# GpSimd's sums of w_out's quarters spread over batch 1's output units, their casts some units behind, and quarter products read in front of later low parts

## The chip, the cores and the metric

One NeuronCore of a Trainium2 chip runs the whole program. The metric is the device time of one execution in microseconds. TensorE (PE in the rows) multiplies, VectorE (DVE), ScalarE (ACT) and GpSimd (POOL) do the elementwise work, and SyncE's queue (SP) issues the DMAs. Each engine works through its own queue in order; semaphores tie the queues together.

## The reference

The inputs are q, k, v of 8 batches, 8 heads, 576 tokens and 64 channels, and the weights of a gated MLP. Attention runs within chunks of 64 tokens; its output, put together to 512 channels a token, is the MLP's input x:

```python
scores = scale * q_c @ k_c^T            # chunks of 64 tokens
out    = softmax(scores) @ v_c          # -> x: (8, 576, 512)
h = gelu_tanh(x @ w_in)                 # (8, 576, 1024)
u, v = h[..., :512], h[..., 512:]
v_n = layer_norm(v) * g_ln
v_s = w_sg @ v_n + b_sg                 # over the tokens of a batch
return x + (u * v_s) @ w_out
```

## The kernel before

**Precision by pairs.** Every operand of a large product is held as a high and a low float32r part (`_h`, `_l` or hi, lo): ScalarE casts the high part, VectorE subtracts it from the source to get the low part (`split`, lines 99 to 104), and TensorE sums three products.

**Units.** A batch's MLP is cut into units of TensorE work with VectorE and ScalarE work behind each: `v_unit` (v half of x @ w_in, GELU, layer norm; 12 products of 512 columns), `u_unit` (u half, GELU into the tile u2; 24 products of 288 columns), `s_unit` (w_sg times the normed v, times u), and the output. In the name v23 the first digit is the batch and the second the number of the unit. v24 takes the first 64 tokens of batches 2 and 3 at once, from the tile xodd, and its layer norm ends in the tiles z1 and z2 (lines 548 to 550). Accumulators are the three PSUM buffers `pm`; a unit can start when one is free, that is when the GELU (or another reader) of the unit three before has run.

**Output, two ways.** Batches 0 and 1 have output units o00 to o13 (`o_unit`, lines 694 to 703), four a batch. From batch 2 on the output is formed by Strassen's scheme from seven products of quarters (`o_product`, named p1, p5, p2, p6, p3, p7, p4 in this order). Their right sides are sums of the gated activations' quarters, made in `gated_quarters`; for p6, p7 and p4 they are split into high and low parts in the tile `tv`. Their left sides ("factors") are quarters of w_out and sums of quarters. `make_factors` (the B steps) forms them once: ten additions or subtractions on GpSimd (line 254), four splits (lines 285 and 286), DMA writes to the DRAM tensor `factors` (lines 261 and 287), and four loads of the first factors into a ring of four places that takes over w_out's tiles (line 245). The sums, and the high and low parts of each split, lie in one tile `sums` that takes the place (tag "u2") that u2 has in other stages; so the first sum waits until s13 has read batch 1's u2, and the GELU of u20, which writes batch 2's u2, waits until `sums` is no longer read.

**Attention.** 36 tiles of 128 tokens: loads (A), scores (S, or P for two tiles) and softmax, transposition of the probabilities (T, on VectorE and ScalarE), output product and its eviction to xh, xl, xf (O, or Q for two; `keep`). The products of tiles 5 and up go into the fixed tile `banks` and into a `pm`. Tile 13 holds the last tokens of batch 2 and the first of batch 3.

**Order.** `START` lists the steps up to batch 2's first three units by hand; then a loop runs over the units of batches 2 to 7, and `SLOTS` says after which unit a piece of attention is traced. The framework keeps data dependences, and orders a queue by the order in which the program traces the work, save that work which it takes to be ready sooner may go ahead. `tc.keep_in_program_order` pins an instruction behind the one traced before it on its engine; all sums, their casts and the factors' writes are pinned, their low parts on VectorE are not. Small tiles share the tag "tmp" with four buffers: the GELU output hs of a v unit, the transposed blocks, the output ot of an output unit.

Of the kernel before, what the change touches and what calls it, by code (L numbers as in the profile page):

```python
# [22 lines left out]
P = 128  # L23
# [6 lines left out]
HS = S // 2  # L30
# [17 lines left out]
v13 Y2 u10 Y3 u11 Y4 u12 Y5 Y6 u13 Y7 A10 s10 A12 s11 P9 s12 s13 T9 o00 T10 P11 o01 o02 o03 Q9 A14 T11 o10 T12 o11 Q11  # L48
S13 A15 o12 T13 o13 P14 A17 B0 B1 v20 B2 v21 O13 B3 v22 B4
# [12 lines left out]
    0: "v1:O4 v3:T5 u0:T6 u1:O56 u1:S78 u3:T7 s0:T8 p7:O78 p7:S9A",  # L62
# [25 lines left out]
def block_attention_gated_mlp(ctx: ExitStack, tc: tile.TileContext, qkv, w_in, w_out, w_sg, g_ln, b_sg, out):  # L88
# [147 lines left out]
    ring, loads, carry = [], [0], []  # L236
# [4 lines left out]
    def load_factor():  # L241
        n = loads[0]
        loads[0] += 1
        if n < 7 * (B - QUARTERS_FROM):
            nc.sync.dma_start(out=factor_place(n).bitcast(F32), in_=factors[n % 7])

    def make_factors(step):

        def quarter(r, c):
            return [a[:, 2 * c : 2 * c + 2, 2 * r * P : 2 * (r + 1) * P] for a in (wout_h, wout_l)]  # L250

        def add(o, a, c, op=ALU.add):
            a, c = (x if x.dtype == F32 else x.bitcast(F32) for x in (a, c))
            tc.keep_in_program_order(nc.gpsimd.tensor_tensor(o, a, c, op=op))  # L254

        sub = lambda o, a, c: add(o, a, c, ALU.subtract)
        (h11, l11), (h12, l12), (h21, l21), (h22, l22) = (quarter(r, c) for r in range(2) for c in range(2))
        if step == 0:
            for p, parts in ((1, (h11, l11)), (2, (h12, l12)), (4, (h22, l22))):
                for a, part in enumerate(parts):  # L260
                    ins = nc.sync.dma_start(out=factors[PRODUCTS.index(p), :, a], in_=part.bitcast(F32))
                    tc.keep_in_program_order(ins)
            flat = mp.tile([P, KT, S], F32R, name="sums", tag="u2").rearrange("p a c -> p (a c)")
            carry.extend(flat[:, i * 4 * P : (i + 1) * 4 * P].rearrange("p (k e) -> p k e", k=2) for i in range(4))
            carry.append(flat[:, 8 * P : 16 * P].rearrange("p (a k e) -> p a k e", a=2, k=2))
            return
        c, d, hi, lo, both = carry
        cf, df, spare = c.bitcast(F32), d.bitcast(F32), lo.bitcast(F32)
        src = cf
        if step == 1:  # L270
            add(cf, h21, h22)
            add(spare, l21, l22)
            add(cf, cf, spare)
        elif step == 2:
            sub(cf, cf, h11)
            sub(cf, cf, l11)
        elif step == 3:
            src = df
            sub(df, h11, h21)
            sub(spare, l11, l21)  # L280
            add(df, df, spare)
        else:
            sub(cf, h12, cf)
            add(cf, cf, l12)
        tc.keep_in_program_order(nc.scalar.copy(hi, src))
        nc.vector.tensor_tensor(lo, src, hi.bitcast(F32), op=ALU.subtract)
        nc.sync.dma_start(out=factors[PRODUCTS.index((5, 6, 7, 3)[step - 1])], in_=both.bitcast(F32))
        if step == 4:
            for i in range(2):
                r = const.tile([P, KT * DM], F32R, name=f"ring_{i}", tag=f"wout_{i}")  # L290
                ring.append(r.rearrange("p (n a k e) -> p n a k e", n=2, a=2, k=2))
            for _ in range(RING):
                load_factor()

# [309 lines left out]
    def gated_quarters(b, dt):  # L604
# [16 lines left out]
        sub(eng, left, left, t1)  # L621
        if dt == 3:
            n = 2 * HS
            tv = mp.tile([P, 8, DH], F32R, name="tv", tag="v").rearrange("p a c -> p (a c)")
            places = [tv[:, i * n : (i + 1) * n].rearrange("p (k c) -> p k c", k=2) for i in range(6)]
            parts = lambda r, j: tuple(quarter_of(a, r, j) for a in (gh[b], gl[b]))
            right.update({1: parts(0, 0), 5: parts(0, 1), 2: parts(1, 0), 3: parts(1, 1)})
            right.update({p: places[2 * i : 2 * i + 2] for i, p in enumerate((6, 7, 4))})
            for p, r, j in ((6, 0, 1), (7, 0, 0), (4, 1, 0)):
                split(*right[p], quarter_of(g, r, j), nc.scalar, nc.vector)  # L630

    def o_product(b, p):
# [27 lines left out]
        if p in (1, 5):  # L660
            kept = held[p] = t("kept")
            add(kept, x(*{1: (0, 0), 5: (1, 1)}[p]))
        elif p == 2:
# [78 lines left out]
    steps["G"], steps["g"], steps["B"] = lambda k: load_w_sg(), split_w_sg, make_factors  # L742
    steps["Y"] = lambda k: o_w(k // 2, k % 2)
    for step in START.split():
        steps[step[0]](int(step[1:]))
    for b in range(2, B):
# [6 lines left out]
        for name in names:  # L753
            if name == "last":
                o_product(b - 1, 4)
                continue
            if b == 2 and name in ("v0", "v1", "v2"):
                continue
            {"v": v_unit, "u": u_unit, "s": s_unit, "p": o_product}[name[0]](b, int(name[1]))
            for f, tiles in slots.get(name, ()):  # L760
                f(*tiles)
# [44 lines left out]
```

## Time and profile before

| | |
|---|---|
| median of three runs | 526.79 us (526.65 to 527.72) |
| the profiled execution | 527.16 us, of which the span from first to last instruction is 525.2 us |
| busy in the span | TensorE 492.5 us (94%), VectorE 386.0 (73%), ScalarE 292.2 (56%), GpSimd 92.4 (18%) |
| granted clock of TensorE | 0.983 of full speed over the span |

A row of the timeline gives start, length, engine, line, operation and tiles, and in brackets how long the engine was idle before it and what ended that. A group of rows with several instructions carries "x" and their count. VectorE's and ScalarE's idle time costs nothing by itself; TensorE's does, when it is not made up.

### The profile page before, as it was taken

To read this page: it belongs to the slowest core of one execution; us is meant where nothing else is said; L and a number is where in the kernel's file an instruction comes from. 1 tells how busy PE (TensorE), PEld (TensorE's weight loads), DVE (VectorE), ACT (ScalarE), POOL (GpSimd) and SP (SyncE) were. 2 spreads that over 40 slices of the span, in tenths; PEclk is the share of its full clock that TensorE was granted. 3 is DMA by queue.
4 is the path that set the end of the run, shared out by engine and by line. 5 is a ranking of instruction groups with operands and counts; after the bars stand their busy time and mean duration, and the time that the engine had idled before them with its cause. 6 is when DMAs were issued, how large, how long until landed. Compare 5 with 4: busy or idle time off the path is not lost.

```text
span 525.2 us, 12508 instructions
## 1 busy us (share of the span) xinstructions
PE 492.5 (94%) x5172; PEld 451.8 (86%) x5172; DVE 386.0 (73%) x783; ACT 292.2 (56%) x535; POOL 92.4 (18%) x94
## 2 busy tenths in 40 slices
PE   5999999999999655999999999999999999999996
PEld 4668897999997545998999889997999889998996
DVE  7998779888767873288868886678758786667156
ACT  5897867644356565126774488328762678333220
POOL 0112000301104651102221131203111131102010
PEclk9999999999999886999999999999999999999999
DMA  8867011154376366059534824078534810082006
GB/s 336 306 176 180 1 41 54 50 137 126 113 234 180 118 213 190 1 161 273 150 95 130 279 81 124 1 235 239 140 105 129 267 54 2 1 278 94 0 2 210
DMA packets 60780, 72.28 MB, mean 138 GB/s; under 512 B 36018, under 2 KB 47794, under 8 KB 60724
## 3 DMA queue, kind: packets, MB, share of 16 engines
q1 hardware_dynamic: 60724, 71.49, 44.9%
q8 instruction: 40, 0.66, 0.5%
q14 instruction: 16, 0.13, 0.1%
HBM read 58.36 MB, written 13.11 MB: 136 GB/s over the span
## 4 chain that ended last, share of the span: by engine, by line
PE 74%; DVE 12%; ACT 6%; POOL 4%; issue 2%; DMA 1%; SPq 0%; POOLq 0%; DVEq 0%; ACTq 0%
PE pm L583 21%; PE pm L563 18%; PE pm L647 13%; PE pm L526 12%; PE pm L694 2%; POOL sums L254 2%; PE banks L396 2%; PE pm L484 2%; PE pm L185 1%; DVE sm L532 1%; DVE blocks L446 1%; ACT L529 1%; DVE xl L104 1%; ACT pt L418 1%; DVE pt L420 1%
## 5 line engine op out<-in xcount | busy, mean ns | idle before, releaser
L583 PE MATMUL pm<-wsg,v 128*128 128x288 f32 x768 | 107.5, 296 | 0.0
L583 PEld LDWEIGHTS pm<-wsg,v 128*128 128x128 f32 x768 | 103.6, 188 | 0.3
L563 PE MATMUL pm<-xh,win_l 128*128 128x288 f32 x256 | 57.4, 306 | 11.9 <-ACT xf L506 6.5
L432 POOL TENSOR_TENSOR pt<-pt,den 128x512 f32<-128x512 f32 x27 | 28.4, 1064 | 191.3 <-DVE den L431 121.1
L535 POOL TENSOR_TENSOR sm<-sm,neg_half 128x1 f32<-128x1 f32 x36 | 36.6, 1015 | 126.2 <-DVE sm L534 122.9
L563 PE MATMUL pm<-xl,win_h 128*128 128x288 f32 x256 | 56.4, 303 | 0.0
L526 PE MATMUL pm<-win_h,xl 128*128 128x512 f32 x128 | 52.4, 409 | 4.1 <-DVE xl L104 2.3
L563 PE MATMUL pm<-xh,win_h 128*128 128x288 f32 x256 | 56.2, 302 | 0.0
L563 PEld LDWEIGHTS pm<-xh,win_l 128*128 128x128 f32 x256 | 42.9, 195 | 13.4 <-ACT xf L506 6.7
L526 PE MATMUL pm<-win_h,xh 128*128 128x512 f32 x128 | 50.8, 397 | 0.0
L526 PE MATMUL pm<-win_l,xh 128*128 128x512 f32 x128 | 50.8, 397 | 0.0
L101 ACT CAST gh<-u 128x576 fp32r<-128x576 f32 x24 | 16.2, 675 | 55.3 <-DVE u L588 27.8
L563 PEld LDWEIGHTS pm<-xl,win_h 128*128 128x128 f32 x256 | 42.6, 195 | 0.0
L563 PEld LDWEIGHTS pm<-xh,win_h 128*128 128x128 f32 x256 | 42.3, 194 | 0.0
L588 DVE TENSOR_TENSOR u<-pm,u 128x576 f32<-128x576 f32 x24 | 18.1, 755 | 30.4 <-PE pm L583 19.1
L543 ACT ACTIVATE v<-hs,sm 128x512 fp32r<-128x512 f32 x32 | 23.2, 724 | 30.5 <-POOL sm L535 29.1
L647 PE MATMUL pm<-gh,ring 128*128 128x288 f32 x192 | 40.1, 294 | 0.0
L449 ACT COPY ptT<-blocks 128x512 f32<-128x512 f32 x31 | 19.0, 619 | 27.3 <-DVE blocks L446 25.7
L526 PEld LDWEIGHTS pm<-win_h,xl 128*128 128x128 f32 x128 | 24.0, 188 | 11.8 <-DVE xl L104 4.5
L647 PE MATMUL pm<-tv,ring 128*128 128x288 f32 x216 | 32.0, 297 | 1.9 <-issue 1.9
L647 PEld LDWEIGHTS pm<-tv,ring 128*128 128x128 f32 x216 | 29.7, 188 | 3.6 <-ACT tv L101 1.6
L544 DVE SCALAR_TENSOR_TENSOR v<-hs,sm,v 128x512 fp32r<-128x512 f32 x32 | 24.9, 778 | 10.0 <-ACT v L543 10.0
(145 smaller groups left out, 1047.9 us busy)
## 6 DMA issues: line engine op xcount, KB each, us to landing
ring<-factors SPq DMA_DIRECT2D x42, 512.0 KB, 4.4
qkv_t<-qkv SPq DMA_DIRECT2D x32, 512.0 KB, 4.7
qkv_t<-qkv SPq DMA_DIRECT2D x124, 64.0 KB, 3.7
out_dram<-u SPq DMA_DIRECT2D x18, 288.0 KB, 5.7
out_dram<-ot SPq DMA_DIRECT2D x14, 288.0 KB, 3.0
qkv_t<-qkv SPq DMA_DIRECT2D x3, 768.0 KB, 11.7
wsg<-w_in SPq DMA_DIRECT2D x4, 512.0 KB, 6.3
wout<-w_in SPq DMA_DIRECT2D x4, 512.0 KB, 7.7
```

The lines of the kernel that those rows point to most:

```text
L101: nc.scalar.copy(hi, src)
L254: tc.keep_in_program_order(nc.gpsimd.tensor_tensor(o, a, c, op=op))
L432: (nc.gpsimd if t > last[1] else pick(f"n{t}")).tensor_tensor(pt, pt, den.unsqueeze(2).broadcast_to([P, H, D]), op=ALU.mult)
L449: nc.scalar.copy(ptT, blocks)
L526: pin(nc.tensor.matmul(pv, a[:, kt, tok], c[:, kt, DH:], start=(i == 0), stop=(i == 11)))
L535: nc.gpsimd.tensor_tensor(rs, rs, neg_half, op=ALU.pow)
L543: nc.scalar.mul(hi, h, rs)
L544: nc.vector.scalar_tensor_tensor(lo, h, rs, hi.bitcast(F32), op0=ALU.mult, op1=ALU.subtract)
L563: pin(nc.tensor.matmul(pm[:, j, :HS], a[:, kt, dc], c[:, kt, j * HS : (j + 1) * HS], start=(i == 0), stop=(i == 11)))
L583: pin(nc.tensor.matmul(pm[:, j, :HS], a[:, dc], c[:, m, j * HS : (j + 1) * HS], start=(i == 0), stop=(i == len(ops) - 1)))
L588: nc.vector.tensor_tensor(g, pm[:, :, :HS], g, op=ALU.mult)
L647: pin(nc.tensor.matmul(pm[:, e, :HS], a[:, k, e * P : (e + 1) * P], c[:, k, :], start=starts and i == 0, stop=i == len(ops) - 1, skip_grou ...
```

## The change

START and SLOTS are reordered: `make_factors` falls into single sums (B0 to B9, one instruction each, traced from o00 to v21), the splits of the sums (C5, C6, C7, each a cast, a low part and two writes, traced after A15, A17 and O13; the fourth, of product 3, after v24), and the six writes of w_out's own quarters (K0, after v22). The high and low parts of a split are two tiles of the tag "tmp" instead of places in `sums`, and a split writes two DMAs of 256 KB where it wrote one of 512 KB. The order of the additions is the same except that the third result has a place of its own and B3 and B4 form h21+h22+l21+l22-h11-l11 in a second place.

In the loop, `split_right(7)` is traced after p1's accumulator has been read and `split_right(4)` after p5's, where all three splits were traced before p1; one subtraction moves likewise. The attention pieces behind p7 of an even batch are traced after v0 of the next batch, and tile O4 of an even batch follows v0 instead of v1.

```diff
-S13 A15 o12 T13 o13 P14 A17 B0 B1 v20 B2 v21 O13 B3 v22 B4
-v13 Y2 u10 ... s13 T9 o00 T10 P11 o01 o02 o03 Q9 A14 T11 o10 T12 o11 Q11
+... s13 T9 o00 B0 T10 P11 o01 B1 o02 B2 o03 Q9 B3 A14 T11 o10
+B4 T12 o11 Q11 S13 A15 C5 B5 o12 B6 T13 o13 P14 A17 C6 B7 v20 B8 v21 O13 C7 B9 v22 K0
...
-    0: "v1:O4 v3:T5 u0:T6 u1:O56 u1:S78 u3:T7 s0:T8 p7:O78 p7:S9A",
+    0: "v0:O4 v3:T5 u0:T6 u1:O56 u1:S78 u3:T7 s0:T8 p7:O78 p7:S9A",
...
+    def sum_step(n):
+        if n == 0:
+            flat = mp.tile([P, KT, S], F32, name="sums", tag="u2").rearrange("p a c -> p (a c)")
+            sums.extend(flat[:, i * 4 * P : (i + 1) * 4 * P].rearrange("p (k e) -> p k e", k=2) for i in range(4))
+        h11, l11, h12, l12, h21, l21, h22, l22 = (a.bitcast(F32) for a in quarters())
+        s1, s2, s3, s4 = sums
+        o, a, c, op = (
+            (s1, h21, h22, ALU.add), (s2, l21, l22, ALU.add), (s1, s1, s2, ALU.add),
+            (s2, s1, h11, ALU.subtract), (s2, s2, l11, ALU.subtract),
+            (s3, h11, h21, ALU.subtract), (s4, l11, l21, ALU.subtract), (s3, s3, s4, ALU.add),
+            (s4, h12, s2, ALU.subtract), (s4, s4, l12, ALU.add),
+        )[n]
+        tc.keep_in_program_order(nc.gpsimd.tensor_tensor(o, a, c, op=op))
+
+    def keep_factor(p, parts):
+        for a, part in enumerate(parts):
+            tc.keep_in_program_order(nc.sync.dma_start(out=factors[PRODUCTS.index(p), :, a], in_=part.bitcast(F32)))
+
+    def split_sum(p):
+        hi, lo = (
+            tmp.tile([P, S], F32R, name="fac", tag="tmp")[:, : 4 * P].rearrange("p (k e) -> p k e", k=2) for _ in range(2)
+        )
+        src = sums[(5, 6, 7, 3).index(p)]
         tc.keep_in_program_order(nc.scalar.copy(hi, src))
         nc.vector.tensor_tensor(lo, src, hi.bitcast(F32), op=ALU.subtract)
+        keep_factor(p, (hi, lo))
+        if p == 3:
...
             for _ in range(RING):
                 load_factor()
+
+    def keep_quarters(_):
+        parts = quarters()
+        for p, i in ((1, 0), (2, 2), (4, 6)):
+            keep_factor(p, parts[i : i + 2])
...
-        sub(eng, left, left, t1)
-        if dt == 3:
+        if dt == 2:
+            sub(eng, left, left, t1)
+        else:
...
-            for p, r, j in ((6, 0, 1), (7, 0, 0), (4, 1, 0)):
-                split(*right[p], quarter_of(g, r, j), nc.scalar, nc.vector)
+            split_right(6)
...
         if p in (1, 5):
             kept = held[p] = t("kept")
             add(kept, x(*{1: (0, 0), 5: (1, 1)}[p]))
+            if p == 1:
+                split_right(7)
+                left, t2 = g[:, 3, :HS], g[:, 1, HS:]
+                nc.vector.tensor_tensor(left, left, t2, op=ALU.subtract)
+            else:
+                split_right(4)
...
+            if (b, name) == (2, "v4"):
+                split_sum(3)
             for f, tiles in slots.get(name, ()):
-                f(*tiles)
+                later.append((f, tiles))
+            if name != "p7" or b % 2:
+                for f, tiles in later:
+                    f(*tiles)
+                later.clear()
```

## Rows read from the trace of the kernel before

**Rows 1.** The page of the profile, parts 1 and 2: busy time of TensorE, and the granted clock in 40 slices of 13.1 us (tenths of full speed).

```profile
PE 492.5 (94%) x5172; PEld 451.8 (86%) x5172; DVE 386.0 (73%) x783; ACT 292.2 (56%) x535; POOL 92.4 (18%) x94
...
PEclk9999999999999886999999999999999999999999
```

**Rows 2.** Whom TensorE waited for between 120 us and the end of the span; columns: us in total, times, longest.

```profile
PE pm L563 <- ACT xf L506: 6.5, 1, 6.5
PE pm L563 <- ACT u L570: 5.3, 1, 5.3
PE pm L526 <- ACT xodd L512: 4.5, 1, 4.5
...
PE pm L526 <- DVE xl L104: 1.4, 3, 1.0
PE pm L526 <- ACT pt L423: 0.7, 1, 0.7
```

**Rows 3.** Busy time of each engine in eight stretches, in this order: units v23, v24, u20, u22 and u23 of batch 2 (each from its first product to the next unit's), then the three idle times of TensorE ahead of v24, u22 and u23. Columns: length, then busy us and instructions of PE, PEld, DVE, ACT, POOL, the granted clock as a share of full speed, DMA share, GB/s.

```profile
168.66:171.57 2.91, 2.91 (x12) 2.17 (x12) 0.66 (x3) 0.00 (x0) 2.83 (x3) 1.00 1.10 327
176.17:180.62 4.45, 4.45 (x13) 3.50 (x14) 3.86 (x6) 1.17 (x2) 2.34 (x2) 0.62 0.01 2
180.62:183.81 3.19, 3.19 (x25) 3.19 (x24) 3.10 (x8) 2.96 (x6) 0.99 (x1) 1.00 0.00 0
195.74:201.01 5.27, 5.27 (x24) 5.19 (x24) 3.57 (x9) 2.92 (x4) 0.79 (x1) 0.58 0.96 315
206.51:211.54 5.03, 5.03 (x24) 5.03 (x25) 0.00 (x0) 1.84 (x4) 0.00 (x0) 0.61 0.03 6
...
171.57:176.17 4.60, 0.15 (x1) 0.00 (x0) 3.66 (x6) 2.91 (x8) 3.89 (x5) 1.00 0.73 267
189.20:195.74 6.54, 0.00 (x2) 0.00 (x1) 4.08 (x7) 2.21 (x5) 3.21 (x3) 0.82 0.77 293
201.17:206.51 5.34, 0.00 (x0) 0.00 (x0) 2.56 (x6) 4.02 (x7) 1.09 (x2) 0.73 0.73 191
```

**Rows 4.** Timeline ahead of unit v24, one engine after the other (GpSimd, ScalarE, VectorE); columns: start us, us, engine, line, operation, out<-in, idle time before it and its releaser.

```profile
167.90 2.52 POOL L254 TENSOR_TENSOR sums<-wout 128x512 f32<-128x512 f32 x2
...
171.82 0.62 ACT L285 CAST sums<-sums 128x512 fp32r<-128x512 f32 x1 [3.48 <-POOL sums L254]
...
175.72 0.41 ACT L512 CAST xodd<-xl 128x256 fp32r<-128x256 f32 x1
...
172.47 1.60 DVE L286 TENSOR_TENSOR sums<-sums 128x512 fp32r<-128x512 f32 x1 [3.15 <-ACT sums L285]
...
174.66 0.41 DVE L104 TENSOR_TENSOR xl<-pm,xh 128x256 fp32r<-128x256 f32 x1
```

**Rows 5.** Timeline ahead of units u22 and u23 (ScalarE, VectorE, SyncE's queue), columns as before.

```profile
187.26 1.26 ACT L549 CAST z<-z 64x512 fp32r<-64x512 f32 x2
...
192.53 0.62 ACT L285 CAST sums<-sums 128x512 fp32r<-128x512 f32 x1 [3.52 <-POOL sums L254]
...
205.81 1.74 ACT L570 ACTIVATE u<-pm 128x576 f32<-128x576 f32 x3
...
198.26 0.68 DVE L286 TENSOR_TENSOR sums<-sums 128x512 fp32r<-128x512 f32 x1
...
198.97 0.32 SPq L287 DMA_DIRECT2D factors<-sums  x1
```

**Rows 6.** Instructions by line: those of the tile sums (lines 254 and 286), and all of line 544; columns: count, shortest/median/longest ns, first and last start.

```profile
L254 POOL TENSOR_TENSOR sums<-sums,wout x3: 1607/1608/1712, 174.2 to 187.9; 128x512 f32<-128x512 f32 x3
...
L286 DVE TENSOR_TENSOR sums<-sums x4: 680/692/1602, 172.5 to 198.3; 128x512 fp32r<-128x512 f32 x4
...
L544 DVE SCALAR_TENSOR_TENSOR v<-hs,sm,v x32: 711/752/1761, 35.7 to 487.1; 128x512 fp32r<-128x512 f32 x32
```

**Rows 7.** Timeline of the places that the moved work comes to (GpSimd, VectorE, TensorE, ScalarE), columns as in rows 4.

```profile
125.21 2.56 POOL L432 TENSOR_TENSOR pt<-pt,den 128x512 f32<-128x512 f32 x2 [20.90 <-DVE den L430]
...
166.89 1.04 POOL L432 TENSOR_TENSOR pt<-pt,den 128x512 f32<-128x512 f32 x1 [2.01 <-DVE den L431]
...
126.79 0.75 DVE L592 TENSOR_TENSOR gt<-pm,u 128x576 f32<-128x576 f32 x1
...
128.28 0.76 DVE L104 TENSOR_TENSOR gl<-gt,gh 128x576 fp32r<-128x576 f32 x1
...
129.14 0.43 PE L694 MATMUL pm<-gl,wout 128*128 128x288 f32 x2
...
164.00 0.63 ACT L423 ACTIVATE pt<-pt 128x512 f32<-128x512 f32 x1
164.92 0.72 ACT L543 ACTIVATE v<-hs,sm 128x512 fp32r<-128x512 f32 x1 [0.29 <-POOL sm L535]
```

**Rows 8.** DMAs of the tensor factors, from issue to landing.

```profile
DMA to landing us min/median/max: 2.6/4.2/8.8
```

**Rows 9.** Timeline of batch 3's quarter products (VectorE, TensorE), and TensorE's wait ahead of v51.

```profile
286.76 0.75 DVE L104 TENSOR_TENSOR tv<-u,tv 128x576 fp32r<-128x576 f32 x1
287.43 0.75 DVE L653 TENSOR_TENSOR kept<-pm,xf 128x576 f32<-128x576 f32 x1
...
288.28 1.83 PE L647 MATMUL pm<-tv,ring 128*128 128x288 f32 x12 [0.61 <-issue]
...
358.87 0.39 PE L526 MATMUL pm<-win_h,xl 128*128 128x512 f32 x1 [0.67 <-ACT pt L423]
```

More of the change, by code (lines that the diff above doesn't have):

```diff
@@ L47 @@
 v02 x1 X2 v03 X3 v04 u00 x2 g0 g1 u01 x3 g2 P5 g3 u02 g4 T5 u03 T6 s00 P7 Q5 s01 s02 T7 T8 s03 v10 Q7 v11 Y0 v12 Y1
-v13 Y2 u10 Y3 u11 Y4 u12 Y5 Y6 u13 Y7 A10 s10 A12 s11 P9 s12 s13 T9 o00 T10 P11 o01 o02 o03 Q9 A14 T11 o10 T12 o11 Q11
-S13 A15 o12 T13 o13 P14 A17 B0 B1 v20 B2 v21 O13 B3 v22 B4
+v13 Y2 u10 Y3 u11 Y4 u12 Y5 Y6 u13 Y7 A10 s10 A12 s11 P9 s12 s13 T9 o00 B0 T10 P11 o01 B1 o02 B2 o03 Q9 B3 A14 T11 o10
+B4 T12 o11 Q11 S13 A15 C5 B5 o12 B6 T13 o13 P14 A17 C6 B7 v20 B8 v21 O13 C7 B9 v22 K0
 """
@@ L235, in block_attention_gated_mlp @@
     factors = nc.dram_tensor("factors", (7, P, 2, 2, 2 * P), F32).ap()
-    ring, loads, carry = [], [0], []
+    ring, loads, sums = [], [0], []
     def factor_place(n):
@@ L245, in load_factor @@
             nc.sync.dma_start(out=factor_place(n).bitcast(F32), in_=factors[n % 7])
[L247 to L284, printed above, removed]
@@ new lines, in quarters @@
+    def quarters():
+        return [
+            a[:, 2 * c : 2 * c + 2, 2 * r * P : 2 * (r + 1) * P] for r in range(2) for c in range(2) for a in (wout_h, wout_l)
+        ]
+    def sum_step(n):
[11 more added lines that the diff above has]
+        tc.keep_in_program_order(nc.gpsimd.tensor_tensor(o, a, c, op=op))
@@ L285, in make_factors @@
+    def keep_factor(p, parts):
[6 more added lines that the diff above has]
+        src = sums[(5, 6, 7, 3).index(p)]
         tc.keep_in_program_order(nc.scalar.copy(hi, src))
         nc.vector.tensor_tensor(lo, src, hi.bitcast(F32), op=ALU.subtract)
-        nc.sync.dma_start(out=factors[PRODUCTS.index((5, 6, 7, 3)[step - 1])], in_=both.bitcast(F32))
@@ L288, in make_factors @@
-        if step == 4:
+        keep_factor(p, (hi, lo))
+        if p == 3:
             for i in range(2):
@@ L628, in gated_quarters, with split_right @@
             right.update({p: places[2 * i : 2 * i + 2] for i, p in enumerate((6, 7, 4))})
-            for p, r, j in ((6, 0, 1), (7, 0, 0), (4, 1, 0)):
-                split(*right[p], quarter_of(g, r, j), nc.scalar, nc.vector)
+            split_right(6)
+    def split_right(p):
+        split(*right[p], quarter_of(u2[0], *{6: (0, 1), 7: (0, 0), 4: (1, 0)}[p]), nc.scalar, nc.vector)
     def o_product(b, p):
@@ L741, in block_attention_gated_mlp @@
     steps["D"] = keep_clock
-    steps["G"], steps["g"], steps["B"] = lambda k: load_w_sg(), split_w_sg, make_factors
+    steps["G"], steps["g"], steps["B"] = lambda k: load_w_sg(), split_w_sg, sum_step
+    steps["C"], steps["K"] = split_sum, keep_quarters
     steps["Y"] = lambda k: o_w(k // 2, k % 2)
@@ L745, in block_attention_gated_mlp @@
         steps[step[0]](int(step[1:]))
+    later = []
     for b in range(2, B):
```

## The prediction

> **What bounds the kernel now.** I read the page first, then TensorE's waits, then the stretches around them. TensorE is busy in 94% of the span and the granted clock is full except in three slices between 170 and 210 us [rows 1]. From 120 us on TensorE has only three long waits, one each of 4.5, 6.5 and 5.3 us; the rest are below 1 us [rows 2]. All three lie in batch 2's first units. So the bound is TensorE's work everywhere but there, and there it is a chain through the sums.
>
> Ahead of v24: GpSimd starts its first sums at 167.90; ScalarE has idled 3.48 us when it can cast the first at 171.82; VectorE has idled 3.15 us when it can form the low part at 172.47, and that takes 1.60 us [rows 4]. Queued behind these two are tile 13's second low part (174.66) and the cast into xodd (175.72), for which v24 waits [rows 2, 4]. Ahead of u22 ScalarE again stands 3.52 us before a cast of a sum (192.53), and behind it are the copies to xf that free the accumulator [rows 2, 5]. Ahead of u23 the wait is for the GELU of u20, 205.81: it writes u2, which has the place of `sums`, and the last read and write out of `sums` start at 198.26 and 198.97 [rows 2, 5].
>
> The idle times are 4.45, 6.54 and 5.34 us, together 16.33 (the first stretch of 4.60 us holds 0.15 of TensorE work) [rows 3]. Each is followed by a unit at a granted clock of 0.58 to 0.62 of the full 2.4 GHz, that is partly at 1.2 GHz: v24 takes 4.45 us where v23 took 2.91, u22 5.27 and u23 5.03 where u20 took 3.19 [rows 3]. That costs 1.54 + 2.08 + 1.84 = 5.46 us more. **What can be won here is 16.33 + 5.46 = 21.8 us**, out of 527.16 us of the profiled execution. That execution is 0.37 us above the median of 526.79; I take differences and set them against the median.
>
> **Part 1: sums and casts moved.** Five of ten sums now stand before the softmax of tile 13, two behind it, and B7, B8 and B9 behind that of tiles 14 and 15, whose last multiplication starts at 166.89 on GpSimd [rows 7]. A sum takes 1.26 us (two in 2.52) to 1.7 [rows 4, 6]. So the first two results are there well ahead of their casts C5 and C6. The third is ready about 167.9 + 1.6 = 169.5, and C7's cast is pinned behind the xodd casts and no longer in front of them. With nothing to wait for, tile 13's second high part, low part and xodd casts follow v22's GELU at about 168.4 and end near 170.5; v23 ends at 171.57 [rows 3]. So v24's wait goes, and with it its slow clock. The small wait ahead of v23 (the largest of the three in the row for xl, 1.0 us) has another cause, casts and table loads of softmax and GELU on ScalarE, and stays.
>
> What is late next is u22, because u20's GELU still waits for `sums`. Times from v24's start T: v24 2.91, u20 and u21 3.19 each, two pieces of attention about 2.2 (from 187.0 to 189.20), so TensorE reaches u22 at T + 11.5 [rows 3]. The last split is pinned behind v24's z casts. These ended at 188.52, 7.90 us after v24's last product at 180.62 [rows 3, 5]. If that lag stays, the split's cast (0.62), low part (0.69) and the GELU (0.65) end at T + 2.91 + 7.90 + 1.96 = T + 12.8, a wait of 1.3 us. Bounds: the lag held 1.0 us of a slow instruction of line 544 (1761 ns against a median of 752) beside sums on GpSimd, and further such ones; without them the wait is 0 [rows 6]. But VectorE was busy without a pause from the end of that first low part, 174.07, and in the new order starts this backlog at 172.47 - 3.15 = 169.32, 4.75 us earlier, while v24 moves by 4.6 and is over 1.54 sooner; C7's low part, as slow as the one it replaces (1.60), comes into the run, and with one low part of 0.69 fewer the z casts end at 184.7, the GELU at 186.6: a wait of 3.5 [rows 4 to 6]. I take the middle, **1.8 us**. The clock after it: full after a wait of 1.0 us (v23: 1.00), 0.62 after 4.45 [rows 2, 3]. 1.8 is nearer the first: 0, at most 2.1. u23 then needs u21's accumulator, whose GELU follows at once: 0.
>
> **Part 2: what the moved work meets.** (a) B0 is pinned behind a multiplication that ends at 127.77 and, after s13's read of u2 (126.79 to 127.54), runs to 129.05. Beside it stands the low part of s13's result, 128.28, which o00 reads at 129.14 [rows 7]. VectorE's low part of a sum beside a sum on GpSimd took 1602 ns against 680 [rows 6]. If it starts only when B0 ends it is done at 129.8: **0.7 us** of TensorE wait; bounds 0 and 0.9. The Trainium skill ("SBUF — State Buffer", section "Who interferes with whom") says that a VectorE instruction with two SBUF inputs and a GpSimd instruction that reads SBUF exclude one another for the whole instruction, whichever starts first. By that rule these 0.7 us are due; without it the sum would be 0.7 us lower. The other sums among the output units lie beside instructions of VectorE that read an accumulator; I cost them at nothing. (b) C6's cast, 0.62 us, comes into ScalarE's row between the exponential at 164.00 and v20's scaling at 164.92, with 0.29 us of slack, ahead of v21's GELU and the cast for v23: **0.4 us**; bounds 0 and 0.62 [rows 5, 7]. (c) Eight tiles more in the four tmp buffers, each held until its write has landed (2.6 to 8.8 us, median 4.2) [rows 8]. C7's pair can hold back the transposed blocks of tiles 14 and 15, which TensorE reads between u21 and u22. Bounds 0 and 4.2; its writes should land near 178, and TensorE needs the blocks near 181, so I take **0.7 us**. (d) SyncE's queue: 14 writes instead of 10, and C5's pair waits there for its low part with the loads for tiles 16 and 17 behind. These are needed only at S78, behind u21: nothing. The reads of the ring start some 15 us before p1 in the new order: nothing.
>
> **Part 3: the loop.** In an odd batch p6 waits 0.61 us instead of 0.16 because VectorE reads p1's accumulator, which p6 goes on with, at 287.43, behind a low part (286.76) that the change traces later [rows 9]. Putting the read in front gives 0.45 us in each of batches 3 and 5: 0.9. The low parts moved behind have p5, p2 and more in front of p7: nothing. The waits ahead of v51 (0.67) and for tile 22's and 31's low parts (1.4 in all less v23's 0.95) lie where O and S pieces move [rows 2, 9]. They may go or return elsewhere: 0.3 of 1.1. Gain **1.2**, bounds 0 and 2.0.
>
> **The sum.** 21.8 - 1.8 - 0.7 - 0.4 - 0.7 + 1.2 = 19.4 us: 526.8 - 19.4 = **507.4 us**. All costs at nothing and all gains: 21.8 + 2.0, or 503.0.
>
> **Rivals.** (1) *The wait moves to u22 in full.* v24's layer norm and the last split queue behind tmp buffers or behind B8 and B9 on GpSimd, and u20's GELU comes as late after TensorE's arrival as a wait of before: 6.54 us and 2.08 of slow clock instead of 1.8 [rows 3]. Then 507.4 + 6.8 = 514.2. For it: VectorE has no pause in that stretch, and the last sums can't start before 167.9 [rows 4, 7]. Against: the cast no longer waits behind the sums one after another.
>
> (2) *The spreading doesn't reach v24.* C7's cast or low part is queued ahead of the xodd chain all the same, since low parts aren't pinned, and the sums that it needs end no earlier than before's first. v24's wait and slow clock come back, 6.0 us: 513.4. Against: the pin on ScalarE.
>
> (3) *Slower: the four tmp buffers fill.* Each v unit's GELU would wait for a split's write to land, with its write held on SyncE's queue behind another split's low part, and TensorE would stop at each of v20 to v24 for 4.2 us and then run at the low clock for 1.5 more [rows 3, 8]: 28 us lost against 21.8 won, 533 us. It decides from the fourth such stop on. Against: in the rows a v unit holds its buffer a few microseconds only, and three units' accumulators cover a late GELU.
>
> (4) *No change:* the waits go but all of it is given back before the end. In batches 3 to 7 TensorE has nothing but waits below 1 us [rows 2], so nothing there can take it back.
>
> **How the numbers follow.** My forecast, 503 to 511 us, has 0.64; rival 1 0.18; rival 2 0.10; slower 0.04; no change 0.02; still faster than 503 0.02. The range of 503.0 to 515.0 takes in the forecast with its bounds and rivals 1 and 2. Within 0.2% is about what a measurement of this kernel can't tell from no change. Faster 0.94, within 0.2% 0.02, slower 0.04.
>
> **What would show it.** Right: no wait of TensorE for xodd ahead of v24; a single wait of 0 to 3.5 us between u21 and u23, ended by u20's GELU; the granted clock full from 160 to 210 us; a wait below 1 us in o00; p6 of batches 3 and 5 waiting 0.2 us. Wrong: a wait for xodd or a GELU of over 4 us, clock shares near 0.6 after it, new waits among o00 to v23 of over 2 us together, or a wait of v20 to v24 for a tmp buffer.

## The result, and the profile after

The changed kernel takes **519.27 us** (median of 4 runs, 519.05 to 519.73), the kernel before in the same session 527.25: a ratio of 0.9849, 95% interval 0.9832 to 0.9866. The change is faster by 1.5%. The forecast was 507.4 us with a range of 503.0 to 515.0: the sign was right, the size was not. About 8 us were gained where 19.4 were forecast. Line numbers shift between the two kernels: in after the attention product (484 before) is L481, units v, u and s are L523, L560 and L580, the GELU of v (529) is L526, the scores (396) L393, the sums L265, the casts and low parts of sums L277 and L278.

Parts 1 and 2 of the page, as in [rows 1]: TensorE is a little busier in its share, and the granted clock still falls in three slices.

```profile
PE 491.1 (95%) x5172; PEld 451.6 (87%) x5172; DVE 385.6 (75%) x783; ACT 288.9 (56%) x533; POOL 90.8 (18%) x94
PEclk9999999999999888999999999999999999999999
```

TensorE's waits between 120 us and the end, as in [rows 2]: us in total, times, longest.

```profile
PE pm L481 <- ACT ptT L451: 5.9, 2, 4.9
PE pm L481 <- ACT hs L526: 2.9, 2, 1.5
PE pm L523 <- ACT hs L526: 2.5, 1, 2.5
PE pm L647 <- ACT ptT L446: 1.2, 2, 0.6
PE pm L580 <- ACT u L567: 0.5, 2, 0.3
```

All three waits of [rows 2] above 4 us are gone, as forecast: nothing waits for xodd or a GELU of u20 any more, and for xf only one product of attention, 0.45 us. In their place stand two that the sum did not have: 4.9 us inside a piece of attention (for the transposed blocks of tile 15) and 2.5 us ahead of v22. Next, the stretches, with the columns of [rows 3]: the wait ahead of v22, then v22, v23, v24 and u20, the wait for tile 15's blocks, the pieces of attention behind it, u22, and u23.

```profile
166.59:169.06 2.47, 0.00 (x0) 0.00 (x0) 1.66 (x5) 2.44 (x5) 1.46 (x2) 1.00 0.92 191
169.06:173.53 4.47, 4.47 (x13) 3.52 (x14) 4.47 (x10) 3.04 (x8) 4.34 (x5) 0.62 0.96 280
173.53:176.30 2.77, 2.77 (x13) 2.23 (x12) 2.12 (x4) 1.73 (x3) 1.93 (x2) 1.00 0.05 20
176.30:179.10 2.80, 2.80 (x13) 2.26 (x12) 2.77 (x8) 0.60 (x1) 0.76 (x1) 1.00 0.73 258
179.10:182.30 3.20, 3.20 (x25) 3.19 (x24) 2.86 (x7) 2.95 (x6) 1.15 (x2) 1.00 1.02 339
186.29:191.19 4.90, 0.00 (x0) 0.00 (x0) 2.52 (x6) 3.98 (x9) 0.00 (x0) 0.92 0.77 278
191.19:194.38 3.19, 3.19 (x97) 2.93 (x97) 0.84 (x2) 1.20 (x3) 0.00 (x0) 0.50 0.96 316
194.38:198.94 4.56, 4.56 (x27) 4.56 (x25) 3.63 (x6) 3.66 (x6) 0.00 (x0) 0.69 1.07 216
198.94:202.14 3.20, 3.20 (x26) 3.20 (x25) 2.05 (x7) 2.24 (x3) 1.71 (x2) 1.00 0.04 8
```

v24 follows v23 without a gap and takes 2.80 us at the full clock. But v22 takes 4.47 us, 1.67 more than v24, and from 191.19 to 198.94 the clock costs some 1.5 (3.19 us for 96 products, of which 94 take 1.62 at the full clock in the run "split behind tile 15" below) and 1.36 (u22's 4.56 against u23's 3.20) more: 2.9. So up to batch 2's first s unit the change puts in 2.48 + 1.67 + 4.90 + 2.9, and 1.41 of two small waits at the product of tiles 11 and 12 (149.16 and 150.91): 13.4 us. It takes out the 21.8 of the forecast and the 0.95 ahead of v23: 9.4 net. By the traces this unit starts at 202.14, before at 211.54, with 0.32 between the two at the start of the multiplications of tiles 9 and 10 on GpSimd (125.53 and 125.21): 9.72. From there to the end after takes 315.4 us, before 313.7: the loop loses 1.7.

**Ahead of v22.** ScalarE and VectorE, columns as in [rows 4].

```profile
163.98 0.63 ACT L420 ACTIVATE pt<-pt 128x512 f32<-128x512 f32 x1 [2.93 <-DVE pt L417]
165.96 0.63 ACT L420 ACTIVATE pt<-pt 128x512 f32<-128x512 f32 x1 [1.35 <-DVE pt L417]
166.50 0.60 ACT L277 CAST fac<-sums 128x512 fp32r<-128x512 f32 x1
...
168.41 1.09 ACT L526 ACTIVATE hs<-pm 128x512 f32<-128x512 f32 x2
...
143.19 2.44 DVE L453 COPY ptT<-blocks 32x256 f32<-32x256 f32 x2 [0.74 <-ACT ptT L446]
...
156.08 0.68 DVE L278 TENSOR_TENSOR fac<-sums,fac 128x512 fp32r<-128x512 f32 x1
...
160.23 1.50 DVE L453 COPY ptT<-blocks 32x256 f32<-32x256 f32 x2 [0.69 <-ACT ptT L446]
...
162.54 0.68 DVE L404 TENSOR_REDUCE nmax<-banks 128x8 f32<-128x512 f32 x1
```

The same of the kernel before, v20's GELU and the maximum of tile 14's scores:

```profile
162.09 0.60 ACT L529 ACTIVATE hs<-pm 128x512 f32<-128x512 f32 x1
...
158.65 0.68 DVE L407 TENSOR_REDUCE nmax<-banks 128x8 f32<-128x512 f32 x1
```

Before, v20's GELU ran between the exponentials of tiles 14 and 15 (160.15 and 164.00). Now both exponentials and C6's cast come first, and the GELU that frees v22's accumulator runs at 168.41. The exponentials are late because VectorE is: tile 14's maximum starts at 162.54 (before 158.65). Going back along VectorE's row, the pairs of copies of tile 11's and tile 13's transposed blocks took 2.44 and 1.50 us (0.58 each before), and C5's low part stands in the middle of tile 13's softmax. GpSimd's row says what lay beside those copies:

```profile
142.83 2.66 POOL L265 TENSOR_TENSOR sums<-sums,wout 128x512 f32<-128x512 f32 x2
...
158.76 2.52 POOL L265 TENSOR_TENSOR sums<-wout 128x512 f32<-128x512 f32 x2
```

The copies from 143.19 and the one at 160.23, beside sums, are the only slow ones. By line (shortest, median, longest ns), first after, then before:

```profile
L453 DVE COPY ptT<-blocks x62: 282/285/1355, 68.3 to 440.3; 32x256 f32<-32x256 f32 x62
```

```profile
L456 DVE COPY ptT<-blocks x62: 282/285/289, 68.1 to 447.2; 32x256 f32<-32x256 f32 x62
```

**Ahead of tile 15's product.** ScalarE and VectorE, then TensorE.

```profile
187.58 0.62 ACT L277 CAST fac<-sums 128x512 fp32r<-128x512 f32 x1
189.01 1.19 ACT L567 ACTIVATE u<-pm 128x576 f32<-128x576 f32 x2 [0.82 <-DVE fac L278]
190.09 0.62 ACT L446 COPY ptT<-blocks 128x512 f32<-128x512 f32 x1
190.74 0.83 ACT L451 COPY ptT<-blocks 32x256 f32<-32x256 f32 x2
...
188.23 0.69 DVE L278 TENSOR_TENSOR fac<-sums,fac 128x512 fp32r<-128x512 f32 x1 [1.11 <-ACT fac L277]
188.84 0.70 DVE L443 STREAM_TRANSPOSE blocks<-pt 128x512 f32<-128x512 f32 x1
...
191.19 1.44 PE L481 MATMUL pm<-ptT,qkv_t 64*64 64x64 f32 x29 [4.90 <-ACT ptT L451]
```

Tile 15's blocks are transposed only behind the last split's low part (188.84; before at 181.35, ahead of it), though VectorE stood idle for 1.11 us just then, and their copies stand on ScalarE behind the split's cast and the GELUs of u20 and u21.

### The profile page after: what moved, and what is told of

It reads as the page before. It is cut to its first block, busy times and chain, and to the rows that moved or that the text cites. A ratio compares the mean times of both kernels' runs of the same rounds, so it can differ in the third digit from the quotient of the medians.

```text
span 517.5 us, 12516 instructions
## 1 busy us (share of the span) xinstructions
PE 491.1 (95%) x5172; PEld 451.6 (87%) x5172; DVE 385.6 (75%) x783; ACT 288.9 (56%) x533; POOL 90.8 (18%) x94
## 4 chain that ended last, share of the span: by engine, by line
PE 62%; DVE 20%; ACT 10%; POOL 2%; issue 2%; DMA 2%; SPq 0%; ACTq 0%; DVEq 0%; POOLq 0%
PE pm L580 17%; PE pm L560 14%; PE pm L523 14%; PE pm L647 9%; PE pm L700 3%; DVE xl L104 2%; PE banks L393 2%; DVE gl L104 2%; PE pm L185 1%; DVE sm L529 1%; DVE ptT L453 1%; DVE pt L417 1%; PE pm L481 1%; DVE v L541 1%; DVE den L426 1%
## 5 line engine op out<-in xcount | busy, mean ns | idle before, releaser
L580 PE MATMUL pm<-wsg,v 128*128 128x288 f32 x768 | 108.0, 297 | 0.5 <-ACT u L567 0.5
L580 PEld LDWEIGHTS pm<-wsg,v 128*128 128x128 f32 x768 | 103.9, 189 | 1.3 <-ACT u L567 1.0
L523 PE MATMUL pm<-win_h,xl 128*128 128x512 f32 x128 | 52.3, 409 | 4.5 <-ACT hs L526 2.5
L560 PE MATMUL pm<-xh,win_l 128*128 128x288 f32 x256 | 56.3, 301 | 0.0
L560 PE MATMUL pm<-xl,win_h 128*128 128x288 f32 x256 | 55.6, 299 | 0.0
L560 PE MATMUL pm<-xh,win_h 128*128 128x288 f32 x256 | 55.5, 298 | 0.0
L523 PE MATMUL pm<-win_l,xh 128*128 128x512 f32 x128 | 51.6, 403 | 0.0
L523 PE MATMUL pm<-win_h,xh 128*128 128x512 f32 x128 | 51.4, 401 | 0.0
L560 PEld LDWEIGHTS pm<-xh,win_l 128*128 128x128 f32 x256 | 41.9, 191 | 1.3
L560 PEld LDWEIGHTS pm<-xh,win_h 128*128 128x128 f32 x256 | 41.6, 191 | 0.0
L560 PEld LDWEIGHTS pm<-xl,win_h 128*128 128x128 f32 x256 | 41.6, 191 | 0.0
L526 ACT ACTIVATE hs<-pm 128x512 f32<-128x512 f32 x36 | 21.1, 595 | 25.7 <-PE pm L523 25.4
L529 DVE BATCH_NORM_STATS2 sm<-hs 128x6 f32<-128x512 f32 x36 | 24.4, 684 | 14.1 <-ACT hs L526 14.1
L523 PEld LDWEIGHTS pm<-win_h,xl 128*128 128x128 f32 x128 | 24.4, 191 | 11.8 <-ACT hs L526 2.9
L104 DVE TENSOR_TENSOR gl<-u,gh 128x576 fp32r<-128x576 f32 x24 | 18.4, 765 | 18.9 <-ACT gh L101 18.9
```

The costliest lines, as they stand in the source:

```text
L104: lo_eng.tensor_tensor(lo, src, hi.bitcast(F32), op=ALU.subtract)
L523: pin(nc.tensor.matmul(pv, a[:, kt, tok], c[:, kt, DH:], start=(i == 0), stop=(i == 11)))
L526: nc.scalar.activation(h, pv, AF.Gelu_apprx_tanh, scale=-1.0)
L529: nc.vector.bn_stats(st, h)
L560: pin(nc.tensor.matmul(pm[:, j, :HS], a[:, kt, dc], c[:, kt, j * HS : (j + 1) * HS], start=(i == 0), stop=(i == 11)))
L580: pin(nc.tensor.matmul(pm[:, j, :HS], a[:, dc], c[:, m, j * HS : (j + 1) * HS], start=(i == 0), stop=(i == len(ops) - 1)))
```

## The experiments

**Two halves.** The first kernel keeps START, the sums and splits of the change and takes the loop from the kernel before; the second is the reverse.

```diff
 # sums only
-    0: "v0:O4 ...
+    0: "v1:O4 ...
-            split_right(6)              # and 7, 4 in o_product
+            for p, r, j in ((6, 0, 1), (7, 0, 0), (4, 1, 0)):
+                split(*right[p], ...)
-                later.append((f, tiles))
+                f(*tiles)
```

> The changed kernel with the loop of before (three splits ahead of p1, attention pieces and tile O4 where they were); only the sums, casts and writes are moved. Theory A, that the loop's part costs time (the waits of 1.35 and 1.53 us ahead of u31 and u51's attention pieces come from it): batches 2 to 7 take 313.7 us from s20 to the end as before and not 315.4, so 1.4 us below the changed kernel, about 517.9. Rival B, that the loop's part gains the 0.9 to 1.2 us forecast and something else costs it: 520.3. Up to s20 both expect the changed kernel's waits (2.5 ahead of v22, 4.9 in the attention piece behind u21).

> The kernel before with the loop's part of the change alone (splits for p7 and p4 behind the reads of p1 and p5, attention pieces behind p7 after the next v0, tile O4 after v0). Theory A: slower than before by 1.4 us, about 528.3, with waits of over 1 us ahead of the attention piece behind u0 in batches 3 and 5, and p6's wait of 0.61 us come back at p7. Rival B: faster by 0.9 to 1.2, about 525.8. Up to s20 both expect the waits of before (4.45, 6.54, 5.34).

Sums only: 516.99 us, ratio to before 0.9795 (0.9767 to 0.9823). Loop only: 530.2 us, 1.004 (1.0026 to 1.0054). The loop part by itself makes the kernel slower, and without it the rest gains some 2 us more; 1.2 of them lie behind batch 2's first s unit in the profiled executions. Up to that unit the first has after's waits (0.47, 0.96, 2.48, 4.90), the second nearly those of before (0.95, 4.43, 6.00, 4.82). So Part 3 of the prediction had the wrong sign.

**Which part of the loop.** Moved low parts and reads as in the change; the pieces of attention at the places of before.

```diff
-    0: "v0:O4 ...
+    0: "v1:O4 ...
-                later.append((f, tiles))
+                f(*tiles)
```

> The changed kernel with the attention pieces where they were before (behind p7 at once, tile O4 after v1) and the splits for p7 and p4 behind the reads. Theory, that the pieces alone cost time in the loop and that the splits neither gain nor lose because the wait of 0.61 us only moves from p6 to p7: the kernel with the sums alone, 517.0, no waits of over 1 us in batches 3 and 5, 0.6 us at p6 or p7 in each of them. Rival, that the forecast 0.9 us of the splits is there: 516.1. Other rival, that the splits cost: 518 or more.

515.63 us, 0.9776 (0.9758 to 0.9794). From batch 2's first s unit to the end it takes 311.9 us, where sums only takes 314.1, after 315.4 and before 313.7: moving the low parts gains, moving the pieces costs. Over all kernels of this study this stretch takes 311.8 to 312.2 in the three with this loop, 313.3 to 314.1 in the three with the loop of before and 314.8 to 315.4 in the six with the change's. By the means the low parts gain 1.7 us and the pieces cost 3.1. Ahead of that unit this kernel, sums only and the change run the same instructions in the same order, and this one is still 1.2 us sooner there: its u22 ran at the full clock, 3.30 us against 4.56 and 4.62. That much of its time is the clock and not the edit. Two batches, from the first s unit of batch 2 to that of batch 4, take 115.0 us here, 116.5 in after, 115.1 before. The place is behind u0 of batches 3 and 5. After, TensorE and ScalarE:

```profile
229.51 1.16 PE L481 MATMUL pm<-ptT,qkv_t 64*64 64x64 f32 x64
246.53 1.16 PE L481 MATMUL pm<-ptT,qkv_t 64*64 64x64 f32 x64 [1.35 <-ACT hs L526]
...
237.05 1.15 ACT L420 ACTIVATE pt<-pt 128x512 f32<-128x512 f32 x2
...
245.90 1.06 ACT L526 ACTIVATE hs<-pm 128x512 f32<-128x512 f32 x2
```

The same with the pieces of before:

```profile
225.86 1.16 PE L481 MATMUL pm<-ptT,qkv_t 64*64 64x64 f32 x64
244.07 1.16 PE L481 MATMUL pm<-ptT,qkv_t 64*64 64x64 f32 x64
...
232.17 1.15 ACT L420 ACTIVATE pt<-pt 128x512 f32<-128x512 f32 x2
...
239.32 0.57 ACT L526 ACTIVATE hs<-pm 128x512 f32<-128x512 f32 x1
...
242.10 0.58 ACT L526 ACTIVATE hs<-pm 128x512 f32<-128x512 f32 x1
```

With `later`, the pieces of an even batch's p7 come behind the next batch's v0 (229.51 instead of 225.86). Their exponentials, table loads and copies then fall among the GELUs of v1 to v3 on ScalarE; the last two of these run together at 245.90, in the other kernel at 239.32 and 242.10 (whose first s unit of batch 2 starts 0.8 us earlier), and the next product behind u0 waits 1.35 us (1.53 in batch 5) for the accumulator that they free. And p6's 0.61 us of [rows 9] were no gain: p6 doesn't wait any more (its read came forward), but p7, some 4 us on, waits 0.61 to 0.68. It goes on with p6's accumulator, and in after VectorE's read of that (283.43, 0.72 us) now stands behind p4's low part (282.14) and a transposition (282.81). The profile names ScalarE's copy of the transposed blocks as releaser, which ends 0.07 us behind the read; p7 doesn't use that copy.

**Tile 15's blocks.** Three theories: the last split's pair is claimed from the four tmp buffers ahead of tile 15's blocks and so comes ahead of them in each queue (own places for the pair end it); the split as such is in the way on ScalarE and VectorE (tracing it later ends it); or tile 15's softmax itself is late.

```diff
 # pair in xodd
-            tmp.tile([P, S], F32R, name="fac", tag="tmp")... for _ in range(2)
+            xp.tile([P, HP, 2 * ODD], F32R, name=f"xodd_{i}", bufs=1)... if p == 3
+            else tmp.tile([P, S], F32R, name="fac", tag="tmp")...
 # split behind T15
-            if (b, name) == (2, "v4"):     # ahead of the slots
+            if (b, name) == (2, "u0"):     # behind them
                 split_sum(3)
```

> The changed kernel, but the last split's high and low part lie in the tiles of xodd, which v24 has read by then, and no longer in two of the four tmp buffers. Theory, that tile 15's transposed blocks stood behind the last split only because that split had taken the tmp buffers first: the transposition runs some 6 us earlier, the wait of 4.90 us in the attention piece behind u21 falls below 1, TensorE then waits 1 to 2 us for u20's GELU ahead of u22, and the slow clock after it goes: 4 to 6 us less, about 514. Rival, that VectorE's backlog sets the transposition's place: no change, 519.3, wait again near 4.9.

> The changed kernel with the last split traced behind tile 15's transposition (after u0 of batch 2) instead of after v24; its pair stays in tmp. Theory, that who asks first for the tmp buffers decides the order: the transposition and its two copies on ScalarE run before the z casts, the wait of 4.90 us behind u21's attention piece goes to below 1, and so does the slow clock behind it; u22 waits up to 2 us for u20's GELU instead; about 513.5, below the kernel with the pair in xodd (515.8), where one copy of tile 15 stayed behind the last cast. Rival, that v24's chain on VectorE sets it: 517 or more.

Pair in xodd: 515.79 us, 0.9767 (0.9741 to 0.9793). The transposition moved up to 184.25 and took all but one of its copies with it; nothing else on VectorE and ScalarE changed its place there, so the claim on tmp does set it. But the last of the blocks' copies still stood on ScalarE behind the z casts and the split's cast, and the waits were 0.24 and 3.57 instead of 4.90. Counted from the multiplications of tiles 9 and 10 it is 3.9 us ahead of after at the first s unit, but only 1.1 of that lie in the wait; 1.5 are the clock at v22, which this edit can't have moved, and 1.3 the clock at u22. Split behind tile 15: 514.9 us, 0.9751 (0.9727 to 0.9775); the wait is 2.09, then 0.43 ahead of u22, and the clock behind them is full. What is left of the wait is again ScalarE's order, here the last copy behind v24's z casts:

```profile
188.19 1.25 ACT L546 CAST z<-z 64x512 fp32r<-64x512 f32 x2
189.45 0.40 ACT L451 COPY ptT<-blocks 32x256 f32<-32x256 f32 x1
```

So the claim on tmp sets the transposition's place and 1.1 us of the wait; with the whole split later, claim, cast and low part, 2.8 of the 4.90 go. The other 2.09 end with a copy that waits in ScalarE's queue, while the transposition was done at 185.35, before TensorE came (187.02): the third theory, a late softmax, isn't needed for them.

**Ahead of v22.** First B1 to B4 right behind B0, away from tile 11's copies; then C6 behind the product of tile 13; then both, with the last split late and in xodd, and the loop of before.

```diff
-... o00 B0 T10 P11 o01 B1 o02 B2 o03 Q9 B3 A14 T11 o10 B4 T12 ...
+... o00 B0 B1 B2 B3 B4 T10 P11 o01 o02 o03 Q9 A14 T11 o10 T12 ...
-... A17 C6 B7 v20 B8 v21 O13 C7 B9 v22 K0
+... A17 B7 v20 B8 v21 O13 C6 C7 B9 v22 K0
```

> The changed kernel with sums B1 to B4 right behind B0, ahead of the softmax of tiles 11 and 12 on GpSimd instead of behind it; nothing else moves. Theory, that a sum on GpSimd holds up VectorE's 32x256 copies beside it for its whole length (1355 ns at most, 289 before) and that this delays the output piece of tiles 11 and 12 and all behind it: the copies of tile 11 take 0.3 us again, the waits ahead of and in that piece (0.45 and 0.96) fall to 0.4 in all, v20 to v22 come 1 to 1.5 us earlier, the wait ahead of v22 shrinks by as much or stays, about 517.8. Copies of tiles 9 and 10 get slower instead, which nobody waits for. Rival, that the delay comes from the order of the queues: same waits, 519.3.

> The changed kernel with the second split (C6) traced behind tile 13's output instead of ahead of v20. Theory, that C6's cast, pinned behind the exponential of tile 15 and ahead of v20's GELU in the claim on tmp, pushes that GELU behind it: the GELU runs between the two exponentials, some 4 us earlier, the wait of 2.48 us ahead of v22 and the slow clock in v22 (1.5 us) go. Of these 4 us up to all are kept: 515.3 if tile 15's transposition moves up as well, 519.3 if the wait behind u21 grows by as much. Rival, that the lateness of tile 13's and 14's softmax on VectorE alone delays that GELU: wait ahead of v22 over 1.5 us still.

> The sums part alone (loop of before) with three changes together: B1 to B4 right behind B0, C6 behind tile 13's output, the last split behind tile 15's transposition with its pair in the tiles of xodd. Theory, that the lost gain lay in these places: below every other kernel so far, between 506 and 512. Rival, that a wait only moves on to the next unit each time: 514 to 516.

Sums ahead of tile 10: 519.32 us, 0.9827 (0.9792 to 0.9862), no difference to the change. Tile 11's copies are back at 0.59 for two, but those of tiles 9 and 10, now beside the sums, took 2.64 and 0.95. C6 late: 521.95 us, 0.9893 (0.9874 to 0.9912), slower than the change. The theory was right about ScalarE: v20's GELU runs between the exponentials again, and v22 starts at 166.91 without a wait. But the wait moved on: 2.87 us ahead of v23, and tile 15's grew to 6.8.

```profile
PE pm L481 <- ACT ptT L451: 7.8, 2, 6.8
PE pm L523 <- DVE xl L104: 2.9, 1, 2.9
```

One of its rows shows the price of the tmp buffers: a GELU of v for which ScalarE waits until a split's write has landed.

```profile
179.64 1.22 ACT L526 ACTIVATE hs<-pm 128x512 f32<-128x512 f32 x2 [1.72 <-DMA factors<-fac]
```

All three: 515.83 us, 0.9778 (0.9762 to 0.9793), with 2.86 ahead of v23, 1.03 ahead of v24, and 0.89 and 2.93 for tile 15. In these two kernels the order on ScalarE only chose which unit waits.

**Together.** The first kernel has the low parts of the change, the pieces of before and the last split behind tile 15. The second adds sums in other places and C5's low part behind tile 13's reciprocal.

```diff
-... o00 B0 T10 P11 o01 B1 o02 B2 o03 Q9 B3 A14 T11 o10
-B4 T12 o11 Q11 S13 A15 C5 B5 o12 B6 T13 o13 P14 A17 C6 B7 v20 B8 v21 O13 C7 B9 v22 K0
+... o00 B0 B1 B2 B3 B4 B5 B6 T10 P11 o01 o02 o03
+Q9 B7 B8 A14 T11 o10 T12 o11 Q11 S13 A15 o12 C5 T13 o13 B9 P14 A17 C6 v20 v21 O13 C7 v22 K0
```

> The changed kernel's START and split_right; attention pieces at the places of the kernel before; the last split traced behind tile 15's softmax, at the end of unit u0 of batch 2. Theory (the costs of the pieces in the loop and of the last split ahead of tile 15 have different places and add): the 3.6 us that leaving out the pieces gave and the 4.4 us that the later split gave both come off 519.3: 511.3 us, 510.3 to 512.3; first unit s of batch 2 near 198, stretches of batches 2 and 4 of 54.5 us and of batch 3 and 5 of 60.5. Rival (the pieces' places also decide what stands around tile 15, so that only one of the two is kept): 514 to 516 us.

> As the run beside it (split_right, pieces of before, last split late), and B1 to B6 right behind B0, B7 and B8 behind the multiplications of tiles 10 and 11, B9 behind that of tile 13, C5's low part behind tile 13's reciprocal, C6 still ahead of v20. Theory (the wait ahead of v22 is the lateness that C5's low part and the sums beside the copies of tiles 11 and 13 put on the softmax of tile 14): its first maximum starts 3 to 4 us earlier than in the changed kernel (162.5), the copies of tiles 11 and 13 take 0.6 us for two again, the wait of 2.5 us ahead of v22 falls to 1.0 or less, v22 runs at the full clock in 2.9 us, and the time is 2.5 to 4 us below the run beside it: 507.3 to 508.8 us. Rival (the wait is C6's cast and the order of GELU and exponentials on ScalarE, or moves on to v23 and v24 as it did with C6 behind O13): less than 1 us below the run beside it, 510.3 or more.

The first: 513.12 us, 0.972 (0.9703 to 0.9738), between the theory and its rival. Up to the first s unit it runs the instructions of "split behind tile 15" in the same order, and it is there no sooner (72.2 us behind the multiplications of tiles 9 and 10, 72.1 there). Its v22 and v23 ran at the full clock, 5.69 us against 7.26, but TensorE then came 2.1 us sooner to tile 15's blocks, which were ready only 0.8 sooner: 0.26 and 2.92 of wait instead of 2.09, and a slow clock behind it. So the pieces' places don't decide this wait. What the loop adds is 2.6 us (312.2 against 314.8) and not 3.6, of which 1.2 had been u22's clock. The second is **the fastest kernel of the study, 510.38 us**, 0.9675 (0.9657 to 0.9694). It is 2.7 us below the run beside it, as its theory had it, but not by the way that the theory named, and its time was missed with that of the run beside it. Tile 14's maximum starts at 162.45, 36.65 us behind the multiplications of tiles 9 and 10, where it was 37.01 in after: 0.4 us earlier and not 3 to 4. GpSimd and VectorE show why:

```profile
128.32 3.04 POOL L265 TENSOR_TENSOR sums<-wout 128x512 f32<-128x512 f32 x2
...
132.81 2.66 POOL L265 TENSOR_TENSOR sums<-sums,wout 128x512 f32<-128x512 f32 x2
...
130.24 2.64 DVE L453 COPY ptT<-blocks 32x256 f32<-32x256 f32 x2
133.59 0.70 DVE L443 STREAM_TRANSPOSE blocks<-pt 128x512 f32<-128x512 f32 x1
134.98 1.94 DVE L453 COPY ptT<-blocks 32x256 f32<-32x256 f32 x2 [0.69 <-ACT ptT L446]
```

Tile 13's copies are free again (0.58), but tile 9's pay 2.06 us, tile 10's 1.36 and tile 11's 1.04. The transposition beside a sum is not slower (0.70): it is the copies. The wait ahead of v22 fell to 1.23 mostly because TensorE arrives 1.0 us later (it waited 0.84 at 143.33 behind the same copies); v22 starts 0.2 us earlier. Most of the gain up to the s unit lies behind it: from v22's start to the first s unit it takes 27.4 us, the kernel beside it 28.6, after 33.1, with no sums left beside the units (a layer norm's instruction with two SBUF inputs, L538, took 1.81 us beside a sum in after, at 171.83, and 0.74 here) and a wait of 2.09 for tile 15. No run freed all the copies at once, so how much of v22's wait is theirs alone stays open.

## Why the prediction was wrong

**Right: what can be won, and Part 1's first half.** The three waits and their slow units are gone, 21.8 us, and v24 runs at the full clock as forecast. The wait ahead of v23, which was to stay, went too (0.95). SyncE's queue cost nothing up to the s units; at the very end (511.64) TensorE waits 0.53 us for a factor's load ahead of its last product, here and with C6 late, and in none of the other kernels.

**The step that failed first: "The other sums among the output units lie beside instructions of VectorE that read an accumulator; I cost them at nothing."** They lie also beside VectorE's copies of transposed blocks, 32x256, from SBUF to SBUF: 2.44 and 1.50 us instead of 0.58. The rule named in the prediction (the Trainium skill, "SBUF — State Buffer", section "Who interferes with whom") counts copies that run in a two-port mode among the instructions that contend with GpSimd, besides those with two SBUF inputs; I applied only the second half of it. That these copies run in such a mode no row says, but their time fits it: low parts take 0.41 us for 256 columns and 0.69 for 512, that is 0.27 to 0.28 for each 256 and some 0.14 besides, and a copy of 256 columns takes 0.285, half as long per column (an estimate from these durations). The pair from 143.19 ends at 145.63, just behind the sums beside it (145.49). The traces agree with the rule in three kernels (the change, sums ahead of tile 10, the fastest one), with 0.95 to 2.64 us for two copies beside sums and 0.58 to 0.60 without. With C5's low part, which I did not weigh at all in its place on VectorE, tile 14's softmax comes 3.6 us late. On the path of that lateness stand the 1.41 us of waits at tiles 11 and 12 and, by the order of ScalarE's queue, v22's 2.48, and the clock took 1.67; how much of these the copies alone make stays open.

**(b) C6's cast.** Sized at 0.4; its own 0.60 us is on the path. With it late the wait ahead of v22 was gone but stood ahead of v23. The term was right as a duration and wrong as a picture: what counts is the lateness that all of this queue carries.

**The step that cost most: (c), the four tmp buffers.** Sized at 0.7, with a bound of 4.2. It was the last split's pair, that of product 3, not C7's, and it cost not by a landing write but by its place: tile 15's blocks come behind it on VectorE and on ScalarE. 4.90 us of wait and some 2.9 of clock, above the bound, which knew neither the queue nor the clock. By the two runs on it the claim on the buffers is the smaller part of that wait (1.1 us, with v22 at another clock); the places of the split and of v24's z casts ahead of the copies are the larger. About 1.7 of the 4.90 (an estimate) are Part 1's wait for u20's GELU, forecast as 1.8: that GELU ends at 189.66, and with the blocks there in time TensorE would have come to u22 at about 186.29 + 1.65 = 187.9. The lag of the z casts behind v24, taken as 7.90, was 8.5 (187.57 against 179.10): that term was near.

**(a) B0's lock** is there (the low part takes 1.36 us, before 0.76) and costs nothing. I had the wrong reader: o00 is an output of batch 0 and the low part is s13's, of batch 1. In after's timeline the read of gl in o00 starts 0.5 us before the low part ends (129.96), so it did not need it, and 0.7 was 0:

```profile
129.46 0.43 PE L700 MATMUL pm<-gl,wout 128*128 128x288 f32 x2
...
128.60 1.36 DVE L104 TENSOR_TENSOR gl<-gt,gh 128x576 fp32r<-128x576 f32 x1
```

The lock that the rule of the Trainium skill foretold was shown, the wait that I hung on it was not.

**Part 3.** Forecast +1.2, measured -1.7 in the two profiles and -1.4 by the means over kernels with the same loop. The low parts gain 1.7 by these means, though p6's 0.61 only became p7's 0.62; some 0.6 of it are TensorE's waits ahead of products (1.9 us in all before, 1.2 to 1.3 with the low parts moved), the rest is not placed. The move of the attention pieces, which I had as 0.3 of gain and called places where a wait "may go or return", costs 1.5 us in each of two pairs of batches (waits of 1.35 and 0.27 in the first, 1.53 and 0.27 in the second): 3.1 in all.

**The sum.** Up to the s units 18.2 were forecast and 9.7 measured, in the loop +1.2 and -1.7: 8.5 + 2.9 = 11.4 of the 11.9 us that are missing; another 0.3 is the later start of after's trace. Of the rivals the first was nearest (a late chain takes the place of the waits, 514.2), but it had one place and there were two, each with its slow clock. The range ended at 515.0 because no case had both.

## What to carry to other kernels

When work moves to GpSimd's idle time, list what VectorE does in that time by operation and operands: a copy from SBUF to SBUF was as exposed here as an operation with two SBUF inputs, and a transposition was not. A tile from a small rotating pool sets the order of the queues, so a new pair claimed ahead of an old tile is an edit of every queue that the old tile passes. A wait that has been removed by reordering one engine's row comes back one unit later if the chain that feeds this row is still late: cost the lateness, not the instruction, and check each removed wait against the next reader on the path.

## What the runs showed of the hardware that I had not expected

A pair of 32x256 copies on VectorE goes from 0.58 to 2.64 us beside a row of 128x512 sums on GpSimd, up to 1369 ns for one (with C6 late). GpSimd's sums themselves took 1277 to 1429 ns in the change, where before four of ten took 1607 to 1712.

The same idle time of TensorE does not always bring the low clock. After 2.47 to 2.49 us ahead of v22 the unit ran partly at 1.2 GHz in the changed kernel (granted 0.62 over the unit) and in three others (sums only, the low parts with the pieces of before, the last split behind tile 15), and at 1.00 with the pair in xodd and in the kernel with the last split behind tile 15 and the pieces of before, whose wait and the two units' first products behind it (columns of [rows 3]) read:

```profile
167.21:169.69 2.48, 0.00 (x0) 0.00 (x1) 1.66 (x5) 2.45 (x5) 1.47 (x2) 1.00 0.79 177
169.69:174.20 4.51, 4.51 (x19) 3.68 (x20) 4.51 (x11) 3.05 (x8) 4.40 (x5) 1.00 0.90 273
```

So some 1.5 us at v22 (with v23, 7.2 us against 5.7), and 1.3 at u22, can be the clock alone between two kernels that run the same instructions up to there. A difference of that size between two kernels' times shows an edit's effect only where the stretch that it changes is read by itself.
